# Loading k and q of one batch behind the fourth gate/val unit instead of inside the second projection

## The chip, the cores and the metric

One core of one Trainium2 chip. The metric is device time in microseconds (us) of a whole run. Each run also has a span, from its first to its last instruction on the core, about 1.8 us shorter than the time, and a mean granted TensorE clock (1.0 is full speed).

## The reference, cut to what matters

```python
# attention: batch 8, heads 8, seq 576, head_dim 64, features 128
phi(x) = exp(h - max h) / sqrt(m),   h = x @ omega.T - |x|^2 / 2
kv = k_p.T @ v ; z = sum(k_p) ; x = (q_p @ kv) / (q_p @ z + 1e-6)
# feed-forward on x as 4608 tokens of 512
out = (gelu(x @ w_gate) * (x @ w_val)) @ w_out        # d_ff 1536
```

## The kernel before

The kernel runs the attention of one batch after the other and weaves it into the feed-forward, which goes in nine tiles of 512 tokens. A batch has 576 tokens, so tile and batch borders don't coincide. After a start-up, a loop handles pairs of batches (b and b+1 for b = 3, 5, 7): two output projections (`out_units`), then two gate/val tiles (`gate_units`). Units of attention work are hung in as side work at numbered places.

k and q of a batch are loaded by DMAs that GpSimd issues and that also cast them to bf16. Each of these loads lands in a double-buffered tile, which is later transposed by DMA.

```python
def load_kq(b, nm, js=slice(0, 4)):
    ...
    nc.gpsimd.dma_start(out=dst[:, js], in_=kq_src(b, nm)[:, js])
...
def kq(b):
    return [(0, lambda nm=nm: load_kq(b, nm)) for nm in "kq"] if b < B else []
```

`nd` computes a block of up to 128 tokens of x, and the SP queue issues a DMA transpose that puts it into the xT tile that the gate/val matmuls read. Output rows leave through the same SP queue.

```python
def nd(b, m, ...):
    ...   # matmuls with q_pT and kz, then reciprocal and multiply on VectorE
        for xt, c, d0, n in x_parts(b * S + m * P, np_):
            nc.sync.dma_start_transpose(out=xt[:, :, c:c + n], in_=x_sb[p0 + d0:p0 + d0 + n])
...
def out_units(t, copy, held=()):
    ...
                copy(o_sb, ps)
                def store():
                    for p0, n, rows in segments(t * T_TOK + qq * P, P):
                        nc.sync.dma_start(out=rows, in_=o_sb[p0:p0 + n, :])
...
for b in (3, 5, 7):
    t = b - 2
    ...
    run(out_units(t, vcopy), kq(b + 2) + [(i, u) for i, u in side if i < 12])
    run(out_units(t + 1, acopy if b + 1 < B else vcopy),
        kq(b + 3) + [(i - 12, u) for i, u in side if i >= 12])
    side = ahead(b + 2, 14)
    if b + 1 < B:
        side += spread(kv_units(b + 1), 3, 4) + spread(nd_units(b + 1), 6, 14)
    run(gate_units(b), sorted(side, key=lambda s: s[0]))
    run(gate_units(b + 1), ahead(b + 3, 2))
```

The units "h" in `side` scale v of batch b+1 on GpSimd (`v_s`).

The softmax here doesn't subtract the row's maximum and nothing guards it: scores larger than these inputs give would overflow.

## Time and profile before

| | before |
|---|---|
| time, median of the first 3 runs | 355.32 us (354.25 to 355.61) |
| profiled run, time and span | 353.49 us, 351.7 us |
| TensorE busy | 342.0 us, 97% of the span |
| waits of TensorE over 1.1 us | one, 1.7 us, for an xT transpose |

TensorE is nearly always busy, so the time is read from the few places where it waits. In the chain of work that ended last, a line that isn't TensorE marks such a place. In the lists of waits, the columns after the colon are the total, the number of waits and the longest one. The lines are in the prediction.

### The profile page before, as it was taken

Reading aid. Unit: us, or ns where it says so; the run is one execution under the profiler, and the core shown is the slowest. Engines: PE = TensorE matmul, PEld = TensorE weight load, DVE = VectorE, ACT = ScalarE, POOL = GpSimd, SP = SyncE. Lnnn points to the kernel's source line nnn. Section 1 sums busy time; section 2 is a strip of 40 time slices with the busy share of each in tenths; the row PEclk is TensorE's granted clock in tenths of the full one; section 3 lists DMA queues with packets and bytes.
Section 4 is the critical chain, followed back from the end, with each engine's and each line's share of the span. In section 5 each row is a group of like instructions: output and inputs, shape, how many; then the busy total and the mean of one; then the engine's idle time right before and its main releaser. Section 6 shows DMA issues by size and latency. Waiting matters only on the chain.

```text
span 351.7 us, 7021 instructions
## 1 busy us (share of the span) xinstructions
PE 342.0 (97%) x2883; PEld 174.2 (50%) x2883; DVE 183.7 (52%) x346; ACT 156.9 (45%) x226; POOL 56.1 (16%) x61
## 2 busy tenths in 40 slices
PE   8899999999999999899999999999999999999995
PEld 6685545455444454454444454544444544444443
DVE  3845669957333448384334557654436553333321
ACT  3964285843334767423336577233357113333000
POOL 6672101060000242200000414000002200000000
PEclk9999999999999999999999999999999999999999
DMA  6999999675999979429999435279003351000144
GB/s 173 267 177 208 206 297 274 84 138 105 198 179 178 136 156 206 89 45 221 114 220 134 105 84 111 52 179 128 0 0 91 72 117 32 1 0 2 31 111 97
DMA packets 64912, 44.14 MB, mean 125 GB/s; under 512 B 42992, under 2 KB 56560, under 8 KB 64880
## 3 DMA queue, kind: packets, MB, share of 16 engines
q1 hardware_dynamic: 50016, 26.42, 39.9%
q0 software_dynamic: 14560, 17.11, 27.8%
q8 instruction: 22, 0.36, 0.4%
q10 hardware_dynamic: 304, 0.16, 0.2%
q14 instruction: 10, 0.08, 0.1%
HBM read 37.78 MB, written 9.44 MB: 134 GB/s over the span
## 4 chain that ended last, share of the span: by engine, by line
PE 90%; ACT 3%; DVE 2%; DMA 2%; issue 0%; POOL 0%
PE gv_ps L394 53%; PE o_ps L427 25%; PE kz_ps L308 3%; PE nd L334 2%; PE pk L189 2%; PE pq L212 2%; DMA xT<-x_sb 2%; ACT k_p L176 1%; DMA omega_f<-in_omega_dram 1%; DVE x_sb L342 1%; PE o_ps L446 1%; ACT q_m L231 1%; ACT q_pT L243 1%; PE t_ps L138 1%; PE t_ps L151 1%; PE warm L180 1%
## 5 line engine op out<-in xcount | busy, mean ns | idle before, releaser
L385 DVE TENSOR_TENSOR gated<-g_gelu,gv_ps 128x512 bf16<-128x512 bf16 x108 | 74.0, 687 | 95.1 <-PE gv_ps L394 92.1
L383 ACT ACTIVATE g_gelu<-gv_ps 128x512 bf16<-128x512 f32 x108 | 64.3, 597 | 131.0 <-PE gv_ps L394 130.9
L394 PE MATMUL gv_ps<-xT,w_gate_sb 128*128 128x512 bf16 (+1 forms) x456 | 110.6, 368 | 1.7 <-DMA xT<-x_sb 1.7
L394 PE MATMUL gv_ps<-xT,w_val_sb 128*128 128x512 bf16 (+1 forms) x456 | 110.4, 368 | 0.0
L427 PE MATMUL o_ps<-w_out_sb,gated 128*128 128x512 bf16 x420 | 97.7, 379 | 0.0
L394 PEld LDWEIGHTS <-w_gate_sb 128*128 128x128 bf16 x456 | 42.9, 98 | 49.8 <-issue 2.1
L394 PEld LDWEIGHTS <-w_val_sb 128*128 128x128 bf16 x456 | 42.6, 98 | 46.6 <-issue 0.3
L427 PEld LDWEIGHTS <-gated 128*128 128x128 bf16 x420 | 38.3, 98 | 46.8 <-issue 5.8
L291 POOL TENSOR_TENSOR v_s<-vf,f 128x1024 bf16<-128x1024 f32 (+3 forms) x14 | 28.0, 2005 | 92.3 <-DVE f L282 60.6
L176 ACT ACTIVATE k_p<-pk 128x1024 bf16<-128x1024 f32 x32 | 31.0, 1027 | 15.1 <-PE pk L189 15.0
L431 DVE COPY o_sb<-o_ps 128x512 f32<-128x512 f32 x27 | 18.6, 688 | 31.6 <-PE o_ps L427 31.1
L214 ACT ACTIVATE q_pT<-pq 128x1024 bf16<-128x1024 f32 x28 | 27.4, 1039 | 4.6 <-PE pq L212 4.6
L342 DVE TENSOR_TENSOR x_sb<-nd,iden 128x512 bf16<-128x512 f32 x40 | 27.7, 692 | 1.4
L334 PEld LDWEIGHTS <-q_pT 128*128 128x128 bf16 x320 | 14.3, 97 | 8.2 <-issue 0.9
L334 PE MATMUL nd<-kz,q_pT 128*128 128x65 bf16 x320 | 15.9, 193 | 0.6 <-ACT q_pT L243 0.3
L279 DVE TENSOR_TENSOR mx<-mx 128x512 bf16<-128x512 bf16 (+5 forms) x45 | 15.0, 332 | 1.5
L341 DVE RECIPROCAL iden<-nd 128x8 f32<-128x8 f32 x40 | 8.1, 202 | 11.4 <-PE nd L334 11.4
L85 POOL DMA_DIRECT2D k_in<-in_k_dram x7 | 5.4, 774 | 53.4 <-DMA kT<-k_in 49.0
L277 DVE TENSOR_TENSOR mx<-k_p 128x1024 bf16<-128x1024 bf16 (+1 forms) x16 | 13.1, 818 | 1.1 <-ACT k_p L176 1.1
L286 POOL CAST v_s<-f 128x36 bf16<-128x36 f32 (+2 forms) x9 | 5.1, 569 | 46.0 <-DVE f L282 31.8
L313 DVE CAST kz<-kz_ps 128x260 bf16<-128x260 f32 x15 | 5.8, 424 | 10.3 <-PE kz_ps L308 10.3
L308 PE MATMUL kz_ps<-v_s,k_p 64*128 64x65 bf16 x576 | 10.4, 190 | 0.6 <-ACT q_m L231 0.6
(75 smaller groups left out, 176.1 us busy)
## 6 DMA issues: line engine op xcount, KB each, us to landing
out_dram<-o_sb SPq DMA_DIRECT2D x70, 128.0 KB, 2.3
vf<-in_v_dram SPq DMA_DIRECT2D x5, 1152.0 KB, 6.5
q_in<-in_q_dram POOLq DMA_DIRECT2D x8, 576.0 KB, 14.6
k_in<-in_k_dram POOLq DMA_DIRECT2D x7, 576.0 KB, 9.7
vf<-in_v_dram POOLq DMA_DIRECT2D x2, 1152.0 KB, 21.7
w_out_sb<-in_moe_w_out_dram POOLq DMA_DIRECT2D x3, 512.0 KB, 19.9
vf<-in_v_dram POOLq DMA_DIRECT2D x2, 576.0 KB, 7.7
w_gate_sb<-in_moe_w_gate_dram POOLq DMA_DIRECT2D x2, 512.0 KB, 7.9
```

Of the source, the lines that this page charges most:

```text
L176: nc.scalar.activation(bt[b].k_p[:, :, c0:c0 + n, :], ps, func=Exp)
L214: nc.scalar.activation(t.q_pT[:, e, 18 * hf:18 * hf + 16, :].rearrange("m (i a) c -> m a i c", a=2), pq.rearrange("m a (i c) -> m a i c", ...
L279: nc.vector.tensor_max(mx[:, :, :, :n], mx[:, :, :, :n], mx[:, :, :, n:2 * n])
L291: eng.tensor_mul(v_s[b % 2][:, :, n0:n1, :D], vv[:, :, n0:n1, :], t.f[:, :, n0:n1, :].broadcast_to((P, 2, n1 - n0, D)))
L308: nc.tensor.matmul(t.kz_ps[e][:, j * DP1:(j + 1) * DP1], t.k_p[es, a, n, :], v_s[b % 2][es, a, n, :], start=(r == 0), stop=(r == R - 1))
L334: nc.tensor.matmul(halves[g][:, hh, :], (q_rows(b)[:, h, r0:r0 + 2, :] if t.x_pe else t.q_pT[:, h % 2, R * (h // 2) + r0:R * (h // 2) + r0 ...
L342: nc.vector.tensor_mul(x_sb.rearrange("p (g h d) -> p g h d", g=2, h=4), wv4[:, :, :, :D], iden.broadcast_to((P, 2, 4, D)))
L383: nc.scalar.activation(g_of[jf], ps, func=Gelu)
L385: nc.vector.tensor_mul(gated_of[t][:, jf, :], g_of[jf], ps)
L394: nc.tensor.matmul(ps[:, c0:c1], w[:, jm, jf * P:(jf + 1) * P], x_tiles[t][:, jm, c0:c1], start=(jm == 0), stop=(jm == N_DM - 1))
L427: nc.tensor.matmul(ps, gated[:, jf, qq * P:(qq + 1) * P], w_out_sb[:, jf, :], start=(jf == 0), stop=(jf == N_DFF - 1))
L431: copy(o_sb, ps)
```

## The change

The intent is to take the loads of k and q of batch b+3 out of the second projection of a pair, where x is being transposed for the next gate/val tile, and to put them into that gate/val tile.

```diff
-            run(out_units(t + 1, acopy if b + 1 < B else vcopy),
-                kq(b + 3) + [(i - 12, u) for i, u in side if i >= 12])
-            side = ahead(b + 2, 14)
+            run(out_units(t + 1, acopy if b + 1 < B else vcopy), [(i - 12, u) for i, u in side if i >= 12])
+            side = [(4, u) for _, u in kq(b + 3)] + ahead(b + 2, 14)
```

## The prediction

> **What bounds the kernel now.** I read the page first, then the waits, then the chain that ended last, and only then the DMA view. On the page I looked at the busy times and at the matmul group that shows idle time.
>
> ```profile
> PE 342.0 (97%) x2883; PEld 174.2 (50%) x2883; DVE 183.7 (52%) x346; ACT 156.9 (45%) x226; POOL 56.1 (16%) x61
> L394 PE MATMUL gv_ps<-xT,w_gate_sb 128*128 128x512 bf16 (+1 forms) x456 | 110.6, 368 | 1.7 <-DMA xT<-x_sb 1.7
> ```
>
> TensorE is busy 342.0 of 351.7 us, so a change that removes no matmul can win at most the 9.7 us between, and most of that lies at the start and the end. The second line says that the gate matmuls waited 1.7 us, all of it for a DMA transpose that fills xT. The list of waits has it as one single wait (times 1, longest 1.7 us). In the chain it sits here:
>
> ```profile
> 136.11 0.26 PE nd L334 x8
> 136.37 0.02 issue
> 136.40 0.22 DVE iden L341
> 136.62 0.02 issue
> 136.64 0.70 DVE x_sb L342
> 137.34 0.02 issue
> 137.36 5.33 DMA xT<-x_sb
> 142.68 0.14 issue
> 142.82 3.61 PE gv_ps L394 x16
> ```
>
> At every other point between 85 and 327 us this chain is TensorE following itself; here alone it leaves TensorE, at the end of the second projection of the pair of batch 3. Gate/val tile 3 (tokens 1536 to 2047) can't start before the first half of block 2 of batch 3 (tokens 1984 to 2047) has been transposed into xT, and that transpose, issued at 137.36, lands at 142.69.
>
> The same code runs for batch 5 one pair later, with the same matmuls but no k and q load (batch 8 does not exist). This is the control that the trace itself offers:
>
> ```profile
> 210.50 0.24 PE nd L334 x8
> 210.75 0.86 PE o_ps L427 x4
> 211.61 0.75 PE pq L212 x6
> 212.36 1.83 PE o_ps L427 x8
> 214.20 0.49 PE nd L334 x16
> 214.68 0.86 PE o_ps L427 x4
> 215.55 0.65 PE gv_ps L394 x3
> ```
>
> From the nd matmuls of block 2 to the first gate matmul it takes 215.55 - 210.50 = 5.05 us there, and 142.82 - 136.11 = 6.71 us in batch 3. The difference, 1.66 us, is the wait.
>
> Next, why the transpose was late. On GpSimd the two loads go out just before:
>
> ```profile
> 125.86 2.33 POOL L291 TENSOR_TENSOR v_s<-vf,f 128x1280 bf16<-128x1280 f32 x1
> 128.13 0.80 POOL L85 DMA_DIRECT2D k_in<-in_k_dram  x1
> 128.93 0.75 POOL L85 DMA_DIRECT2D q_in<-in_q_dram  x1
> 136.06 1.90 POOL L291 TENSOR_TENSOR v_s<-vf,f 128x1024 bf16<-128x1024 f32 x1 [6.38 <-issue]
> ```
>
> In the DMA view k lands 7.1 us after its issue (135.2) and q 9.7 us after (138.6). The next two fences are that view's rows for the xT transposes, first from 128.1 to 142.8 us (batch 3), then from 202.7 to 215.5 us (batch 5); the last number is the median from issue to landing.
>
> ```profile
> xT<-x_sb SPq DMA_TRANSPOSE x5, 5.3
> ```
>
> ```profile
> xT<-x_sb SPq DMA_TRANSPOSE x4, 2.4
> ```
>
> One by one, the transposes issued at 132.5, 133.8, 137.4 and 138.6 took 6.6, 7.7, 5.3 and 4.2 us; every one of batch 5 took 2.3 or 2.4. The table of windows agrees: DMA share 1.17 at 132.5 to 137.4 us (above 1 because overlapping packets are summed), against 0.29 in the matching window of batch 5, 206.9 to 211.8 us.
>
> **What the Trainium skill says.** "DMA: Bandwidth & Descriptors", section "Issuing engines are not separate DMA queues", says that DMAs of all issuing engines run on the same 16 DMA engines and interleave. The trace agrees: loads from the GpSimd queue and transposes from the SP queue stretch each other, 5.3 against 2.4 us. The same page, "Queues, rings and completion order", says that a DMA's semaphore increment is a strongly ordered write, landing only after every earlier write of that engine across its queues. That is a reason for a small transpose to be held up by a large load; the trace shows the delay, not this mechanism. "Perfetto Trace Analysis", section "DMA Instruction — SWDGE (GPSIMD)", warns that the end the profiler gives for a GpSimd DMA is the end of descriptor generation. It agrees here: 0.80 us in the GpSimd row, 7.1 us to landing. "SBUF — State Buffer", in its box on the "DVE blocks DMA" trap, says certain VectorE modes keep GpSimd from writing descriptors. I use it for a rival below; the two issues took 0.80 and 0.75 us where the shortest of the kernel took 0.74, so no sign of it.
>
> **The change, part by part.** The diff changes an expression in a loop over three pairs, but k and q of batch b+3 exist only for b = 3. So exactly two DMA instructions move, the loads for batch 6. The comparison of the two instruction orders confirms it: TensorE, ScalarE and SP have the same sequence, VectorE the same operations under renumbered buffers, and on GpSimd the two loads go from before the three v_s operations of batch 4 to behind them. Their waits are the same as before (the transposes that read batch 4's k and q, long done) and none is on TensorE, so "behind the fourth unit" does not hold them to a gate unit; they go as soon as GpSimd is through with batch 4.
>
> - Removed from the second projection: 1.18 MB (1056 packets on the GpSimd queue) in flight from 128.1 to 138.6 us. Effect: the transposes should land in about 2.4 us as in batch 5. The one that binds then lands at 137.36 + 2.4 = 139.8. TensorE would otherwise arrive at 136.11 + 5.05 = 141.16, so there are 1.4 us of slack and the wait goes altogether: **-1.66 us**.
> - GpSimd: its work for batch 4 waits for the factors f from VectorE (ready at 135.94 and 140.46), not for the 1.55 us of issuing, after which it was idle 6.38 us. It ends as before at 140.76 + 2.33 = 143.09: 0 us. The kz matmuls that need it start at 146.43 - 1.66 = 144.77, still behind it.
> - Added behind it: k issued at about 143.1, q at about 143.9. The DMA share is only 0.34 at 142.8 to 150.3 us, so by the kernel's other landing times (7 to 10 us where the queues are shared) k lands by 150, q by 153. The transposes of blocks 3 and 4 of batch 3 (142.0, 143.3) and perhaps the first of batch 4 (from 151.6, earlier by 1.66) may stretch from 2.4 to 5 to 8 us. They feed gate/val tile 4, whose first matmul is at 166.07 - 1.66 = 164.4; even 153 + 8 = 161 is in time: 0 us.
> - Readers of the loads: k of batch 6 is transposed from 172.79 on, over 20 us after landing: 0 us.
>
> Behind 142.82 the chain is TensorE alone to 345 us, so the gain is carried to the end. Sum: -1.66 us, 0.47% of 355.32, hence **353.7 us**.
>
> **Rivals.**
> 1. The wait is due to the stores and not the loads. Ten output stores left SP back to back from 121.9 to 130.1 us in batch 3, because SP was busy with transposes up to 121.9. Batch 5's ten left from 191.4 to 204.4, also in a row, and its transposes took 2.4 us, which speaks against it. The last transposes were still slow (4.2 us, issued 138.6) when q had just landed, which says that a backlog and not the load alone plays in. If only half goes, the transpose lands at 141.2 and the gain stays near 1.6 us; if none goes, 355.3.
> 2. The load collides in its new place, with the transposes and stores of the gate/val tile. For it: up to seven xT transposes start in that tile. Against it: the slack above. If one came too late by 2 us, the change would be a wash, 355.3 to 356.
> 3. Another engine takes over at once. When gate/val tile 3 starts 1.66 us earlier, ScalarE still has its 1.28 us table load at 141.84 and the last o_sb copy ahead of the first GELU. In batch 5 the same sequence cost TensorE nothing (7.50 us busy of the 7.50 us from 215.5). If it did cost 0.5 us, 354.2.
> 4. Descriptor writing is slowed by VectorE at the new time. It would delay landing, with 20 us to spare: no effect.
>
> **Range and chances.** The centre is 355.32 - 1.66 = 353.66, given as 353.7. The three runs before span 354.25 to 355.61, 1.36 us, nearly as much as the effect; the profiled execution took 353.49. So the range is 352.4 (gain plus run scatter) to 355.3 (no gain). 2% is 7.1 us. Faster than that is ruled out, as the only mid-kernel wait is 1.66 us: 0.01. Slower by it needs a new wait of more than 7 us in a stage that has slack: 0.01. Same: 0.98.
>
> **What would show it right or wrong.** Right: the gate group's idle before it falls from 1.7 to about 0; the chain runs from o_ps straight to gv_ps at about 141.2; the xT transposes from 132 to 139 us land in about 2.4 us; k_in is issued at about 143; TensorE stays at 342 busy with the span near 350.0. Wrong: the transposes stay above 4 us though the loads are gone (rival 1), a wait on xT appears at the start of gate/val tile 4 near 164 us (rival 2), or the first units of tile 3 wait for GELU (rival 3).

## The result, and the profile after

| | before | after |
|---|---|---|
| median of 6 runs | 355.47 us (354.25 to 356.36) | 353.28 us (352.85 to 354.78) |
| ratio, with 95% interval | | 0.9945 (0.9918 to 0.9971) |

A ratio here is always the mean time of one kernel's fast runs over the mean of the other's fast runs of the same rounds, so it isn't quite the ratio of the medians. "Fast" leaves out single runs that the record marks slow (over 1.5% above the fastest of their kernel). Each later set of rounds has its own runs of before. 353.28 us lies in the range of 352.4 to 355.3, and the difference of the medians is 2.19 us against 1.66 predicted.

Three views of the changed kernel answer those shown of before. The busy line and the gate group of its page:

```profile
PE 342.0 (97%) x2883; PEld 174.2 (50%) x2883; DVE 184.0 (52%) x346; ACT 157.3 (45%) x226; POOL 55.6 (16%) x61
L394 PE MATMUL gv_ps<-xT,w_gate_sb 128*128 128x512 bf16 (+1 forms) x456 | 110.6, 368 | 0.0
```

The gate matmuls no longer wait: 0.0 us where there were 1.7. The chain of work at the same place:

```profile
137.66 0.24 PE nd L334 x8
137.91 0.86 PE o_ps L427 x4
138.77 0.76 PE pq L212 x6
139.53 1.83 PE o_ps L427 x8
141.36 0.49 PE nd L334 x16
141.85 0.86 PE o_ps L427 x4
142.71 3.45 PE gv_ps L394 x16
```

It runs through on TensorE: 142.71 - 137.66 = 5.05 us, the very figure of the control pair. GpSimd's timeline (start, duration), and the xT transposes issued from 127 to 144 us with their median landing time:

```profile
142.31 2.33 POOL L291 TENSOR_TENSOR v_s<-vf,f 128x1280 bf16<-128x1280 f32 x1
144.58 0.80 POOL L85 DMA_DIRECT2D k_in<-in_k_dram  x1
145.38 0.75 POOL L85 DMA_DIRECT2D q_in<-in_q_dram  x1
```

```profile
xT<-x_sb SPq DMA_TRANSPOSE x5, 2.5
```

The loads leave as soon as GpSimd has scaled v of batch 4, and the transposes are back at 2.5 us, from 5.3.

The table of windows of both kernels shows where the DMA work went (columns: window, length, busy time of TensorE, its weight loads, VectorE, ScalarE and GpSimd with instruction counts, then granted clock, DMA share and GB/s). Before:

```profile
0.00:20.00 20.00, 16.34 (x254) 13.13 (x255) 11.57 (x24) 12.81 (x17) 13.95 (x23) 1.00 0.98 208
128.00:143.00 15.00, 13.34 (x203) 7.24 (x202) 10.06 (x24) 11.90 (x16) 5.99 (x6) 1.00 1.04 169
143.00:166.00 23.00, 23.00 (x208) 11.60 (x207) 12.65 (x23) 7.29 (x13) 0.09 (x1) 1.00 0.50 113
```

After:

```profile
0.00:20.00 20.00, 15.33 (x231) 12.11 (x232) 10.95 (x21) 11.72 (x16) 12.12 (x22) 0.91 0.94 201
128.00:143.00 15.00, 15.00 (x212) 8.06 (x211) 9.41 (x24) 10.37 (x15) 4.50 (x4) 1.00 0.38 82
143.00:166.00 23.00, 23.00 (x208) 11.54 (x207) 13.44 (x24) 8.83 (x14) 3.13 (x3) 1.00 1.00 178
```

The DMA share moves from 1.04 and 0.50 to 0.38 and 1.00, and TensorE fills the first of the two windows.

One thing doesn't fit the prediction. It expected a span near 350.0, and the span is 351.4 against 351.7. The first window says why: in the first 20 us, before the change has any effect, TensorE did less (15.33 against 16.34 us busy) at a lower granted clock (0.91 against 1.00). Behind it is a wait of TensorE for the load of q of batch 0, 3.0 us in the profile of after and 0.3 us in that of before. The instructions up to that point are the same in both kernels, so the profile of before had simply caught a good start. Its own timed runs are slower than its profiled one (354.25 to 356.36 against 353.49 us), and in 8 of the 13 profiles below the profiled run is the fastest of its kernel's runs listed with it, so the profiles don't show the typical run. The experiments had to tell this scatter from the gain.

### The profile page after: what moved, and what is told of

It reads as the page before. It is cut to its first block, busy times and chain, and to the rows that moved or that the text cites. A ratio compares the mean times of both kernels' runs of the same rounds, so it can differ in the third digit from the quotient of the medians.

```text
span 351.4 us, 7021 instructions
## 1 busy us (share of the span) xinstructions
PE 342.0 (97%) x2883; PEld 174.2 (50%) x2883; DVE 184.0 (52%) x346; ACT 157.3 (45%) x226; POOL 55.6 (16%) x61
## 4 chain that ended last, share of the span: by engine, by line
PE 91%; DMA 3%; DVE 2%; ACT 2%; POOL 0%; issue 0%
PE gv_ps L394 53%; PE o_ps L427 26%; PE kz_ps L308 3%; DMA q_in<-in_q_dram 3%; PE nd L334 3%; PE pq L212 2%; PE pk L189 2%; DMA omega_f<-in_omega_dram 1%; PE o_ps L446 1%; DVE x_sb L342 1%; PE t_ps L151 1%; ACT k_p L176 1%; PE pq L180 1%; PE t_ps L230 1%; PE pq L240 0%; DVE kT_pe L155 0%
## 5 line engine op out<-in xcount | busy, mean ns | idle before, releaser
L313 DVE CAST kz<-kz_ps 128x260 bf16<-128x260 f32 x15 | 5.8, 423 | 10.6 <-PE kz_ps L308 10.6
L308 PEld LDWEIGHTS <-k_p 64*128 64x128 bf16 x576 | 9.5, 94 | 1.8 <-issue 1.3
```

The source lines that it names most:

```text
L308: nc.tensor.matmul(t.kz_ps[e][:, j * DP1:(j + 1) * DP1], t.k_p[es, a, n, :], v_s[b % 2][es, a, n, :], start=(r == 0), stop=(r == R - 1))
```

## The experiments

**The theory**: the transposes wait behind the DMA work of the two loads, TensorE waits for one of those transposes, and the loads are harmless in their new place. **Rivals**: the wait was chance and the gain is start-up luck. The stores cause the delay, not the loads. It is the exact new place that counts. Or the delay depends on a load being there at all rather than on how much is queued.

The profile of every kernel can be cut into three pieces, which together are its span: the **head** up to the nd matmuls of block 2 of batch 3, then 5.05 us of work plus the **wait** (start of gate/val tile 3 minus head minus 5.05), and the **rest** (spans are printed to 0.1 us, so it is good to 0.05). The last two columns are TensorE's wait for q of batch 0 and the granted clock in the first 20 us.

| kernel | head | wait | rest | wait for q 0 | clock, 0 to 20 us |
|---|---|---|---|---|---|
| before | 136.11 | 1.66 | 208.88 | 0.3 | 1.00 |
| before_again | 136.88 | 1.99 | 208.88 | 2.4 | 0.91 |
| after | 137.66 | 0.00 | 208.69 | 3.0 | 0.91 |
| after_again | 136.53 | -0.01 | 208.73 | 0.6 | 1.00 |
| after_third | 138.38 | 0.00 | 208.67 | 2.0 | 0.83 |
| old_place_no_stores | 135.92 | 0.80 | 208.83 | 0.5 | 1.00 |
| later_still | 136.08 | 0.00 | 208.77 | 2.0 | 0.91 |
| only_k_stays | 138.75 | 0.00 | 208.70 | 2.3 | 0.86 |
| only_q_stays | 137.36 | 0.00 | 208.69 | 2.7 | 0.91 |
| load_in_pair_5 | 136.10 | 0.00 | 208.75 | 0.4 | 1.00 |
| between_scalings | 135.45 | 0.04 | 208.86 | 1.2 | 1.00 |
| old_place_with_v | 136.83 | 3.44 | 210.28 | 1.5 | 0.83 |
| q_first | 135.28 | 0.00 | 208.67 | none | 1.00 |

### 1. Before, again (no edit)

> The kernel before, unchanged, for a second profile and for the scatter. Theory (the two loads delay the xT transposes): ratio 1.000 within 0.003; in the profile again one wait of TensorE of 1.3 to 2.0 us for an xT transpose ahead of gate/val tile 3, and xT landings of 5 to 8 us among those issued 132 to 139 us. Rival (the wait in the first profile was chance, and the measured gain is start-up luck): no such wait this time. Open besides: whether the first 35 us scatter by 1 to 2 us from run to run, as the first two profiles suggest (TensorE busy 31.3 against 30.0 us there).

Measured: ratio 0.9991 (0.9935 to 1.0048). In its list of TensorE waits:

```profile
PE gv_ps L394 <- DMA xT<-x_sb: 2.0, 1, 2.0
```

The wait for xT is back, 2.0 us, with transposes of 4.6 to 8.1 us. It isn't chance. The start scatters too: the wait for q of batch 0 was 2.4 us here and 0.3 us in the other profile of the same kernel. The six runs went from 351.15 to 356.82 us, more than three times the effect.

### 2. After, again and a third time (no edit)

> The changed kernel again. Theory: ratio about 0.995 (1.66 of 355), no wait of TensorE for xT anywhere, transposes of the second projection of the first pair in 2.3 to 2.7 us. Rival (start-up luck): ratio within 0.002 of 1.

Measured: ratio 0.9979 (0.9933 to 1.0026), no wait for xT, the transposes that count in 2.3 to 2.6 us. The expected 0.995 is inside the interval, and so is 1.

> The change a third time, for the size of its gain on the same chip as the larger dose. Theory: no wait for xT; ratio 0.995, pooled with the two earlier measurements between 0.994 and 0.998. Over the runs of one kernel the span should fall by about 2.6 us for each 0.01 of mean granted clock, as fitted on the runs so far, and at equal clock the change should be 0.7 to 1.7 us below before.

Measured: ratio 0.9979 (0.9923 to 1.0034), no wait, transposes 2.3 to 2.5 us. The three ratios have a mean of 0.9968, or 1.1 us. Fitted over the runs of all kernels, a run's span falls by 2.7 us for each 0.01 of mean granted clock, with one line for all. At equal clock the three measurements of the change lie 1.25, 0.87 and 1.07 us below before (standard error 0.31 each).

The clock records of the traces show what lies behind this mean. Before the last matmuls, a lower clock is always 0.50, for 3.41 us or twice as long, 6.83 us. By estimate, 3.41 us at half clock in a span of about 352 lower the mean by 0.005, and the profiles follow this: 0.995 with one such stretch (after), 0.989 with two in a row (after_third), 0.999 to 1.000 with none. So much of the scatter may be how many stretches a run had; for the runs without a trace this isn't shown.

### 3. Old place, without the stores of tile 1 (wrong result)

```diff
                 if part == 2:
                     ...
-                if qq in held:
+                if t == 1:
+                    pass
+                elif qq in held:
                     later.append(store)
```

> Loads in the old place, but the stores of output tile 1 (eight DMAs that leave just before the transposes) are dropped; the result of that tile is wrong on purpose. Theory (the loads are the cause): the transposes still take 4 to 8 us and TensorE still waits 1 us or more before gate/val tile 3, time about as before (0.995 to 1.001). Rival (the backlog of stores is the cause): transposes 2.4 us, no wait, ratio about 0.995 or below.

Measured: ratio 1.0019 (0.997 to 1.0068). The transposes took 6.6, 5.9, 4.5 and 3.5 us (6.6, 7.7, 5.3 and 4.2 in before). The chain at the end of the projection:

```profile
137.78 1.71 PE o_ps L427 x8
139.49 0.93 ACT q_pT L214
140.42 0.63 issue
141.05 0.60 ACT o_sb L431
141.65 0.12 issue
141.77 3.61 PE gv_ps L394 x16
```

The chain names ScalarE's copy of o_sb as what ended the wait. That is a coincidence in time: the binding transpose, issued at 137.2, landed 4.5 us later, at about 141.7, the end of that copy. The timeline of later_still shows the gate without a wait:

```profile
140.97 1.03 PE L394 MATMUL gv_ps<-xT,w_gate_sb 128*128 128x512 bf16 x4
```

The first gate matmul started at 140.97, before the same copy even began (141.21), so the gate doesn't need the copy. (The chain puts this start at 141.13, the modelled end of the o_ps matmuls before it. Matmuls overlap by 0.16 us there, which matters below.) In old_place_no_stores TensorE waited 0.80 us, half of before. Both sides were partly wrong: the loads alone delay the transposes and make TensorE wait, but in this one profile, without the stores of tile 1, only half as long (0.80 us, where the theory said 1 us or more). The stores alone, as in every profile of the changed kernel, leave the transposes at 2.3 to 2.6 us.

### 4. The loads further back still

```diff
-            side = [(4, u) for _, u in kq(b + 3)] + ahead(b + 2, 14)
+            side = ahead(b + 2, 14)
...
-            run(gate_units(b + 1), ahead(b + 3, 2))
+            run(gate_units(b + 1), kq(b + 3) + ahead(b + 3, 2))
```

> The change, with the two loads moved yet further, to the head of gate/val tile 4 in program order. GpSimd has no wait between the two places, so theory: issue time as in the change, right behind the scaling of batch 4 (about 143 us), no wait, ratio 0.995 as after_again. Rival (it is the exact place that counts, or the load collides with transposes of the gate/val tile): a time that differs from after_again by 0.3% or more.

Measured: ratio 0.9962 (0.9918 to 1.0006), no wait. The loads left at 143.02 and 143.82 us, right behind the scaling, like those of the change. Moving them by twenty units in the program changed nothing, as GpSimd has nothing to wait for in between.

### 5. One of the two loads stays

```diff
-                kq(b + 3) + [(i - 12, u) for i, u in side if i >= 12])
-            side = ahead(b + 2, 14)
+                [(i, lambda: load_kq(6, "k")) for i, _ in kq(b + 3)[:1]] + [(i - 12, u) for i, u in side if i >= 12])
+            side = [(4, lambda: load_kq(6, "q")) for _ in kq(b + 3)[:1]] + ahead(b + 2, 14)
```

> Half the dose: the k load of batch 6 stays in the old place, the q load moves as in the change. Theory (transposes wait for the DMA work that is still queued): k alone lands about 7 us after its issue at about 128, i.e. before 135.5; the first two transposes stretch to 3 to 5 us, the one that binds (issued about 137.3) lands in 2.3 to 3 us, and TensorE does not wait for xT. Rival (a GpSimd load anywhere in the projection costs the wait, or the bytes count and half of them cost half): a wait of 0.8 us or more before gate/val tile 3.

> The other half: q stays in the old place, k moves. The same numbers as with k staying, since it is issued at the same moment with the same bytes: no wait for xT, transposes issued at 132 to 134 us in 3 to 5 us, the binding one in 2.3 to 3 us. Rival (q is the one that matters because it lands later): a wait of 1 us or more.

Measured: ratios 0.9968 (0.9889 to 1.0047) and 0.9964 (0.9901 to 1.0027). With k staying it landed 6.6 us after its issue at 130.77, and the transposes took 3.3, 2.4, 2.3 and 2.3 us. With q staying it landed in 8.2 us from 129.31, and they took 4.3, 3.6, 2.3 and 2.3. TensorE didn't wait for xT in either. Half the dose doesn't cost half the wait; it costs nothing, as the load has landed (at 137.3 and 137.5) before the binding transpose is issued (at 140.0 and 138.6). Which of the two stays doesn't matter.

### 6. The same loads in the pair that had none

```diff
+    def load_again():
+        for nm in "kq":
+            again = ld.tile([P, NS, D], BF16, name=f"{nm}_in")
+            nc.gpsimd.dma_start(out=again.rearrange("p (j r) d -> p j (r d)", r=R), in_=kq_src(6, nm))
...
-            run(out_units(t + 1, ...), [(i - 12, u) for i, u in side if i >= 12])
+            run(out_units(t + 1, ...), ([(0, load_again)] if b == 5 else []) + [(i - 12, u) for i, u in side if i >= 12])
```

> The change, with the same two loads issued once more (into dead buffers, never read) at the head of the second projection of the pair of batch 5, the place and moment that the change vacated for batch 3. Theory: the transposes of that projection (issued 206 to 212 us) go from 2.4 to 5 to 8 us; the second of them, issued about 208.2, is the last that gate/val tile 5 needs (tokens 2560 to 3071 end in the first half of block 1 of batch 5), so it lands at about 208.2 + 7.5 = 215.7 against TensorE's arrival at about 215.3: a wait of 0 to 1 us, less than the 1.7 to 2.0 us of batch 3 because one block fewer is needed. Rival (load and transposes do not share anything; something else in batch 3 made it slow): transposes stay at 2.4 us.

Measured: ratio 0.9963 (0.9897 to 1.0029). The loads left at 200.70 and 201.50. The transposes issued at 205.1, 206.4, 207.7 and 210.3 took 6.7, 5.5, 4.5 and 2.9 us, where they had taken 2.4. So the loads put the same delay into a pair that had been clean. TensorE didn't wait: the last transpose that gate/val tile 5 needs was issued at 206.4 and landed at 212.0, and the tile starts at 213.71. The slack of 1.8 us is that of a tile that needs one block fewer.

### 7. The loads between the two scalings of batch 4

This edit is against the kernel before.

```diff
-            run(out_units(t + 1, ...), kq(b + 3) + [(i - 12, u) for i, u in side if i >= 12])
+            run(out_units(t + 1, ...), sorted([(5.5, u) for _, u in kq(b + 3)] + [(i - 12, u) for i, u in side if i >= 12], key=lambda s: s[0]))
```

> The loads placed between the first and the later scaling of batch 4 on GpSimd, so that they leave at about 138 us, when the binding transpose (issued about 137.3) is already under way. Theory: the first transposes are clean (2.4 us); the binding one is hit late or not at all, lands in 2.4 to 4.5 us, and TensorE waits 0 to 0.8 us. Rival (the wait needs the load anywhere in the second projection): a wait of 1.5 us or more as before.

Measured: ratio 0.9951 (0.9882 to 1.002). The loads left at 137.23 and 138.03. The transposes issued at 131.9, 133.2, 136.7, 138.1, 141.0 and 142.5 took 2.5, 2.4, 3.7, 7.2, 7.2 and 6.0 us. The binding one is the third; it landed at 140.4, just when TensorE came, and the wait was 0.04 us. The loads are in the second projection and cost next to nothing, because they left 0.5 and 1.3 us behind the binding transpose. They still stretched it, from 2.3 to 3.7 us, so what is queued shortly behind a transpose counts too, but less: with both loads ahead it took 5.3 and 5.7 us. The slow ones behind it feed the next tile.

### 8. A larger dose in the old place

```diff
-                kq(b + 3) + [(i - 12, u) for i, u in side if i >= 12])
-            side = ahead(b + 2, 14)
+                kq(b + 3) + ([(0, lambda: load_v(5, nc.gpsimd))] if b == 3 else []) + [(i - 12, u) for i, u in side if i >= 12])
+            side = ahead(b + 2, 14)[1 if b == 3 else 0:]
```

> A larger dose on the kernel before: k and q of batch 6 in the old place, and v of batch 5 (as many bytes of source as the other two each) taken from its later place and issued right behind them, so half as much again is queued in the second projection. Result correct. Theory: the transposes there stretch to 7 to 12 us, the binding one lands at about 143 to 147, TensorE waits 3 to 6 us instead of 1.7 to 2.0, and the time follows one for one: 1 to 4 us above before, ratio 1.003 to 1.012. Rival (the transposes wait for the GpSimd queue's issue or for a fixed effect of two queues, not for the queued bytes): wait unchanged near 1.7, ratio within 0.002 of 1.

Measured: 360.37 us against 356.14, ratio 1.0158 (1.0099 to 1.0218), verdict unclear; one of the six runs is marked slow. The runs listed as fast give only 1.0128, or 4.6 us, and which runs the recorded ratio took isn't on record. Either way the time lies above the 1.003 to 1.012 that was expected. The transposes took 10.6, 9.6, 7.1 and 6.2 us, and TensorE's wait was 3.4 us, as expected. Two things differ from the two other loads: v comes in as f32, so the DMA view gives 1152 KB for it where k and q have 576 KB each, and the edit moves its load from the SP queue to GpSimd's.

The wait grew by 1.45 to 1.8 us over the two profiles of before, but the time by 4.2 to 5.6. The table of windows shows where part of the difference is (third column from the end: granted clock):

```profile
141.16:144.57 3.41, 0.72 (x4) 0.10 (x2) 1.59 (x5) 2.03 (x3) 2.50 (x2) 1.00 1.02 193
144.57:147.98 3.41, 2.66 (x7) 1.01 (x8) 0.00 (x0) 0.60 (x1) 0.00 (x0) 0.50 0.73 160
```

The chain has the same stretch as

```profile
145.32 4.91 PE gv_ps L394 x16
```

TensorE stopped at 141.88, the clock went to 0.50 at 144.57 and back to 1.00 at 147.98. Sixteen gate matmuls took 4.91 us, instead of 3.61 behind a shorter wait. These 1.30 us are nearly all of the excess of its "rest" in the table (210.28 against 208.83 to 208.88 in the other profiles with a wait). The Trainium skill, "TensorE: Matmul & The Clock Gate", section "What's actually happening", says that the clock is at half after at least one idle window of about 3.4 us, and full again after about as long a busy one. The trace agrees with the length of the stretch, 3.41 us. But TensorE wasn't idle for so long when the clock fell: 2.7 us had passed since its last matmul, and in the 3.41 us before the fall it was busy for 0.72 us. So the wait's length alone doesn't say whether the clock will fall. The waits of 1.66 and 1.99 us in the two profiles of before were followed by a clock of 1.00.

In this one profile the wait thus cost its own length and another 1.30 us. Of the 4.2 to 5.6 us, 1.1 to 2.9 stay unexplained. The six runs had mean clocks of 0.974 to 0.988, where those of all other kernels had 0.983 to 1.000, so longer waits or more stretches at half clock in other runs are likely, but they weren't seen. Fitted as in experiment 2, its runs lie 3.1 us above before at equal clock (standard error 0.3), so not all of the excess is the clock.

### 9. q of batch 0 earlier, on top of the change

This one follows from the scatter of the start, not from the change.

```diff
+        load_kq(0, "q")
         nc.gpsimd.tensor_scalar_mul(omega_bf, omega_f, scale)
         cast(0, "k", 5, 9, nc.gpsimd.tensor_copy)
-        load_kq(0, "q")
```

> The change, with the load of q of batch 0 issued on GpSimd ahead of the scaling of omega and the cast of k, i.e. about 3 us earlier (1.3 instead of 4.3 to 4.8). Looked for because six of the profiles show TensorE waiting 1.2 to 3.0 us for that load near 11 us. Theory: q lands by about 8 to 9 instead of 11 to 13.5, that wait goes, the first k load is delayed by at most 1 us because it shares the engines, and the time falls 0.5 to 2 us below the change. Rival: k, which everything waits for first, is delayed by as much as q is early, and the time is the same or worse.

Measured: 353.55 us, ratio 0.9947 (0.9895 to 0.9999) against before, where the change itself had 0.9979 in the same rounds. q was issued at 1.4 instead of 4.2 to 4.8 us, landed at 9.5 (4.3 + 9.2 = 13.5 in the profile of after), and the wait for it was gone. It has the shortest head of all profiles, 135.28 us. But the intervals overlap, and at equal clock it doesn't lie below the change (-0.74 against -1.06 us on average, standard error 0.31). That comparison takes out the clock, which this edit may itself have raised: its runs had 0.988 to 1.000, those of after_third in the same rounds 0.985 to 0.995. It is the best candidate among these kernels, not a shown improvement.

## Why the prediction was right

- **The bound and the wait.** Right. Twelve further profiles show a wait for xT ahead of tile 3 in every kernel with both loads queued in front of the binding transpose, and none above 0.04 us where they weren't.
- **The cause.** Right, and sharper now. The delay was induced in the clean pair (experiment 6), removed by half the load (5), removed but for 0.04 us by issuing behind the binding transpose (7), and grew with a larger load (8). What inside the DMA engines holds the transposes up stays open, as the prediction says. Its "stretch each other" is shown for one side only: the transposes stretched, but k and q landed after 7.1 and 9.7 us in before, and no sooner in the new place (7.2 and 10.9).
- **GpSimd and the new place.** Right. The loads left right behind the scaling, at 144.58 (a head later by 1.55 us than in before, so 143.0 on the prediction's clock). The transposes issued at 144.4 and 151.3 took 6.2 and 5.6 us, within the 5 to 8 foreseen. q landed 10.9 us after its issue, about 1.7 us later than the "by 153" on that clock, which cost nothing. No wait appeared at tile 4.
- **Rival 1, the stores.** Half right. It was weighed by the control pair, where stores alone did no harm, and that was correct. The prediction suspected a backlog besides the loads but gave it no part of the 1.66 us. With the loads present, the stores of tile 1 made up about half of the wait (0.80 us without them, in one profile, 1.66 and 1.99 with them).
- **Rivals 2 to 4.** None appeared. A first unit of tile 3 waiting for GELU would show in "rest", which is 208.67 to 208.77 us in the no-wait profiles, and 208.86 in between_scalings, where the next point accounts for it. For rival 4 the prediction calls 0.74 us the shortest DMA issue on GpSimd; one load of v took 0.73, which changes nothing.
- **The size.** The mechanism was right, and the size is less sure than one number says. The traces give 1.66 and 1.99 us of wait, plus about 0.16 us: the first sixteen gate matmuls and what lies between them took 3.61 us in the chain after a wait and 3.45 without one. The timelines say why. Without a wait the first gate matmul starts 0.16 us before the modelled end of the o_ps matmul ahead of it (140.97 against 141.13 in later_still). After a wait, even the 0.04 us of between_scalings, this overlap is lost. The prediction's sum of -1.66 us leaves it out. The times give 0.9945, 0.9979 and 0.9979; so the 2.19 us of the first comparison were on the lucky side, and each of the two repeats gives about 0.7 us, with 1 inside its interval. Over all eight measurements without the wait (the change three times, later_still, the two halves, pair 5, between_scalings) the mean ratio is 0.9964, or 1.3 us; the two controls that keep a wait, before_again and old_place_no_stores, have 0.9991 and 1.0019. At equal clock these eight lie 0.85 to 1.25 us below before, 1.0 on average, which is less than the wait in the traces. They share runs of before, so they aren't independent. The gain is about 1 to 2 us, 1.66 is among them, and the runs don't settle it closer.
- **The span.** The step that failed: "the span near 350.0" took the head of one profile for the head of all. Heads scatter from 135.45 to 138.75 us among the twelve profiles with the same start (all but q_first), and the profile of after drew a slow one, 1.55 us behind that of before. So two single spans (351.7 and 351.4) would have hidden nearly all of the gain. The prediction's range was centred on the timed median, not on the span, and this kept it right.

## What to carry to other kernels

When a small transfer feeds the bounding engine, look at what is queued on the DMA engines ahead of it, from any issuing engine, and move large loads behind it; one of two loads can be free where both cost, if it has landed before the transfer is issued. Use another iteration of the same code in the same trace as a control: it gives the size of a wait without a second kernel. And when the effect is 0.5% and the start scatters by 1%, compare the piece of the trace in which the change acts, not two spans.

## What the Trainium skill lacked or had wrong

- "DMA: Bandwidth & Descriptors", section "Rules for kernel authors", says that a transpose next to ordinary DMAs needs nothing. That is about correctness. For time these runs show it needs room: 2.3 to 2.6 us beside stores alone, 3.5 to 6.6 beside two loads without those stores, 4.2 to 8.1 beside both, and 6.2 to 10.6 with a third load. No page has such numbers.
- The same page doesn't say that the delay isn't in proportion to the bytes ahead: the binding transpose took 2.3 us with one of the two loads in the old place, as with none, and 5.3 and 5.7 us with both. TensorE's wait was 0 us and 1.66 and 1.99.
- "TensorE: Matmul & The Clock Gate" names an idle window of about 3.4 us as what lowers the clock, but not how idle it must be. In these profiles the clock fell eight times before the last matmuls, and TensorE was never idle through the 3.41 us before: it was busy for 15 to 52% of them (21% in the middle of old_place_with_v). The single wait nearest to the fall was 1.5 to 3.0 us long near 11 us, and 2.7 us had passed of the one in the middle. Waits of up to 1.2 us near 11 us left the clock at 1.00, and so did the 1.66 and 1.99 us in the middle of the two profiles of before. No run here was made to find the limit.
